# Two transformer layers on one core: the output projection of the two-layer steps, dimension-major against token-major in units of 32 tokens

## The chip, the cores and the metric

The kernel runs on one core of a Trainium2 chip. A core has a matrix engine (PE, with its weight loads PEld listed apart), a vector engine (DVE), a scalar engine (ACT), a general engine (POOL) and a queue engine that issues transfers (SP). PE reads from the large on-chip memory and writes its results into accumulation banks (PSUM), of which the kernel uses eight, each of 512 fp32 columns over 128 partitions. DVE and ACT read the banks and write back to the large memory. The metric is the device time of one execution in microseconds; less is better.

## The reference, cut to what matters

Two layers, each of an attention over segments with a recurrent memory and of a gated feed-forward part. There are 2048 tokens of 448 dimensions, 16 heads of width 256, 64 segments of 32 tokens, and 8 memory tokens. A segment's memory is the projected output of the segment before it at the memory's places:

```python
for s in range(n_seg):
    h = jnp.concatenate([mem, xs], axis=1)          # 8 + 32 tokens
    q, k, v = h @ Wq, h @ Wk, h @ Wv                # per head
    p = softmax(mask(q k^T * scale))
    o = einsum('bhte,hed->btd', p v, Wo)
    mem = o[:, :M, :]                               # goes into the next segment
    outs.append(o[:, M:, :])
...
x = x + A(layernorm(x)); x = x + B(layernorm(x))    # B: relu(x Wg) * (x Wu) then Wd
x = x + A(layernorm(x)); x = x + B(layernorm(x))
```

The same weights serve both layers. The 64 steps of the memory are a chain: no segment can begin its memory part before the one ahead of it has projected its output.

## The kernel before

**Weights.** Once, at the start, the kernel multiplies Wq with Wk and Wv with Wo per head (`A_sb`, `A3`, `A3z` for the scores, `B_sb` for the output). After that, each head's attention works on the hidden vectors themselves. `B_sb[:, hf, t, :]` holds, for half `hf` of the heads (0 or 1) and tile `t` of 28, a 128 x 448 block of the fused output weight.

**Steps.** `step(g, ff)` (L751) handles segment `g` of layer 1 ("chain 0") and segment `g - 4` of layer 2 ("chain 1") together; there are 68 steps, and those with g from 4 to 63 have both chains. Every odd step also carries a `Feed` (L466): residual, layer norm and feed-forward of one block of 64 tokens of each layer, and loading and storing of those blocks. A step's order on PE is written out by hand, since every matmul is chained to the one before (`in_order`, L74). On the other engines the planner orders instructions by when their inputs are ready, except where `keep_in_program_order` pins an instruction behind the one traced before it on its engine.

**Inside a two-chain step.** Twelve banks of projections (`prj`), whose results ACT and DVE copy to `TQ` and `TZ`; scores of the memory tokens (`Sm`) and of the segment (`Sx`), softmax on DVE and ACT; weighing of the hidden vectors by the probabilities (`weigh_m`, `weigh_m_rows`, `weigh_x`: tiles `ya`, `yb`, `ym`, `y`), whose results are copied into `Y` or `Z`; and the output projection. `YY[hf]` is a pair of buffers, Y for even steps and Z for odd ones, each of 28 tiles by 80 columns: 32 of chain 0, 16 of memory tokens (from `M0` = 32), 32 of chain 1. The segment's columns are written at the end of a step for the next step (`kept`, L844), the memory's in the step itself.

**The output projection before.** `project_out` (L877) has the weight as the stationary operand and 80 columns of `Y` as the moving one: 28 tiles x 2 halves x 3 blocks of 128 output dimensions, 168 matmuls into one bank `ox`. `project_tail` (L929) does the last 64 dimensions in 56 matmuls on two column halves of the array, into the bank `o3`, with copies by ACT and additions by DVE to bring the halves together. The output comes out dimension-major, so the memory tokens can be copied straight into the next step's input `hT` (`finish`, L950; `set_mem`, L228; `project_tail` for the last dimensions). The segment's output goes to `OT`, and at the next odd step `flip_out` (L479) transposes it back on PE, so that `residual` (L482) adds it to the tokens. `weigh_x(1, ...)` is the last thing that a step puts on PE, behind the projection.

**What lies beside.** In an odd step the projection is dealt out between the pieces of the feed-forward part: 10 tiles ahead of `gate_up`, the tail ahead of `down`, the rest behind `down`, with `flipped(PX[1])`, `norm2` and `feed_on` in between (L1113 to L1141). In an even step it stands in four pieces (L1162 to L1179). Banks come from a pool of seven (`ps`) and one more with the tag `ox`, which the projection's bank shares with the bank `c0` of projections and with one of the two banks that `flip_banks` (L176) takes.

**Token-major code that is there already.** The last step does its output in units of 32 tokens on four column tiles, with 32 tokens of `Y` or `Z` stationary and 224 columns of `B_sb` moving (`project_tokens` L962, `add_tokens` L972). Each of its two units has a bank of its own. Steps 1 to 3, which have one chain, project 40 tokens at a time on two column tiles (`project_rows` L891) and transpose the result back on PE (`finish_rows` L918).

Of the kernel before, what the change touches and what calls it, by code (L numbers as in the profile page):

```python
# [54 lines left out]
def build_kernel(ctx, tc, A_x, A_mem0, A_Wq, A_Wk, A_Wv, A_Wo, B_W_gate, B_W_up, B_W_down, out,  # L55
# [29 lines left out]
    def tr(*a):  # L85
        in_order(nc.tensor.transpose(*a))  # L86
# [89 lines left out]
    def flip_banks():  # L176

        return [psum.tile([P, 8, 64], BF, name=f"flip{r}", **where)
                for r, where in enumerate((dict(tag="ox", bufs=1), dict(tag="ps")))]

    def flipped_dims(two, at, src):

# [35 lines left out]
    def rows_in(eng, b, c, src):  # L218

        x = slice(HX[c], HX[c] + SEG)  # L220
        evac(eng, chunks(b)[:, :, 0:4, x].transpose([0, 2, 1, 3]), src.rearrange("p k (s t) -> p k s t", t=SEG))

    def mem_cols(g, cs):
        b, j = divmod(g, BLK)
# [1 line left out]
        return h[:, :, cs[0]:cs[-1] + 1, 0:MEM]  # L226

    def set_mem(g, src, cs, n=4):  # L228
        nc.vector.tensor_copy(mem_cols(g, cs)[:, 0:n], src)


    def idle(n):
# [217 lines left out]
    YY = [[main.tile([P, NT, W], BF, name=f"{name}{hf}") for name in "YZ"] for hf in range(2)]  # L450
    for hf in range(2):
        nc.gpsimd.memset(YY[hf][0][:, :, 0:SEG], 0.0)
    xT = main.tile([P, NPASS, 128], BF, name="xT")
# [8 lines left out]

    part = main.tile([P, 2, DM], F32, name="part")


    class Feed:  # L466

# [21 lines left out]
        def norm(self, eng=None):  # L489
            self.xn = normed(self.st, eng)  # L490

        def xposed(self, other=None):
            tps = transpose_tokens(self.xn)
            r = nc.vector.tensor_copy(xT[:, 0:4, self.n], tps[:, :, self.n])
            if other is not None:
                behind(r, other)
            return tps

        def xposed_rest(self, tps, pin=False, rs=(0, 1)):
            for r in rs:  # L500
                i = nc.scalar.copy(xT[ROWS[r], 4:NPASS, self.n], tps[ROWS[1 - r], 0:3, self.n])
                if pin:
                    tc.keep_in_program_order(i)

        def gate_up(self, u):
            n = self.n
            gps = psum.tile([P, 2, 128], F32, tag="ps", name="gps")
            ups = psum.tile([P, 2, 128], F32, tag="ps", name="ups")
            for i in range(NPASS):
                for e in range(2):  # L510
                    f = 2 * u + e
                    for r, ps in enumerate((ups, gps)):
                        mm(ps[:, e, n], Wgu_sb[ROWS[r], i, f * 128:(f + 1) * 128], xT[ROWS[r], i, n],
                           start=(i == 0 and e == 0), stop=(i == NPASS - 1), skip_group_check=True)
# [236 lines left out]
    def step(g, ff):  # L751
# [5 lines left out]
        cols = [(0, 32) if c == 0 else (48, 80) for c in xs] + [(32, 40) if c == 0 else (40, 48) for c in ms]  # L757
        lo, hi = min(a for a, _ in cols), max(b for _, b in cols)
        if g == 0:
            lo = 0  # L760
# [8 lines left out]
            return YY[hf][(g + later) % 2]  # L769

        def flips_of_rows():
            two = flip_banks()
# [40 lines left out]
        def weigh_m(hf, hk, PT):  # L813
            if not ms:
                return
            ya = psum.tile([P, 256], F32, tag="ps", name="ya")
            for kd in range(2):
                mm(ya[:, kd * 128:kd * 128 + 128], hk[:, kd, :], PT[:], start=True, stop=True)
            nc.scalar.copy(ys(hf)[:, 0:16, M0:M0 + 16], ya[:].rearrange("p (t q) -> p t q", q=16))  # L819
# [4 lines left out]
            nc.vector.tensor_copy(ys(hf)[:, 16:28, M0:M0 + 16], yb[:].rearrange("p (t q) -> p t q", q=16))  # L824

        def weigh_m_rows(hf, hk, PT):
            pt = PT[:, 0:128].rearrange("p (t c m) -> p t c m", c=2, m=MEM)
            y = {c: psum.tile([P, NT * MEM], F32, tag="ps", name=f"ym{c}") for c in ms}
            for kd in range(3):
                for c in ms:  # L830
                    rows = slice(64 * c, 64 * c + L)
                    mm(y[c][:, kd * 64:kd * 64 + 64], hk[rows, kd, :], pt[rows, :, c, :], start=True, stop=True)
            for eo in range(2):
                for c in ms:
                    rows = slice(64 * c, 64 * c + L)
                    mm(y[c][:, 192:224], hk[rows, 4 + eo, :], pt[rows, 4 * eo:4 * eo + 4, c, :], start=(eo == 0),
                       stop=(eo == 1))
            for c in ms:
                evac(nc.scalar if c == 0 else nc.vector, ys(hf)[:, :, M0 + MEM * c:M0 + MEM * c + MEM],
                     y[c][:].rearrange("p (t m) -> p t m", m=MEM))  # L840

        def weigh_x(hf, hk, PT):

            kept = ys(hf, 0 if last else 1)  # L844
            xo = (None, XO[1] - SEG) if g == nseg + LAG - 2 else XO

            def keep(eng, c, t0, src):
                n = src.shape[-1] // SEG
                dst = kept[:, t0:t0 + n, xo[c]:xo[c] + SEG]
                k = max(1, n // 8)  # L850
                r = evac(eng, dst.rearrange("p (k i) (e q) -> p k e i q", k=k, q=16),
                         src.rearrange("p (k e i q) -> p k e i q", k=k, e=2, q=16))
                if eng is nc.vector and hf == 1 and t0 == 0:
                    tc.keep_in_program_order(r)
# [13 lines left out]
            for c in chains:  # L868
                keep(nc.scalar if c == 0 else nc.vector, c, 16, y2[c][:, 0:256])
                tail = y2[c][:, 256:512].rearrange("p (o e i q) -> p e i o q", o=2, e=2, i=4)  # L870
                for e in range(2):
                    rows = slice(64 * e, 64 * e + 64)
                    evac(nc.vector if c == 0 else nc.scalar,
                         kept[rows, 24:28, xo[c]:xo[c] + SEG].rearrange("p i (o q) -> p i o q", q=16),
                         tail[rows, e])

        def project_out(hf, t0, t1):  # L877

# [39 lines left out]
        def finish_rows(mt):  # L918
# [2 lines left out]
            for kd in range(4):  # L921
                tr(tps[:, kd, 0:L], mt[0:L, kd * 128:kd * 128 + 128], ident[0:L, 0:L])
            if ms:
                m = M0 + MEM * ms[0] - lo
                set_mem(g + 1, tps[:, :, m:m + MEM].unsqueeze(2), ms)
            for x, ot in outs():
                nc.vector.tensor_copy(ot, tps[:, :, x.start - lo:x.stop - lo])

        def project_tail():  # L929

# [6 lines left out]
            nc.scalar.copy(swap[0:64, lo:hi], o3[64:128, lo:hi])  # L937
            nc.scalar.copy(swap[64:128, lo:hi], o3[0:64, lo:hi])
            if ms:
                both = slice(M0 + MEM * ms[0], M0 + MEM * (ms[-1] + 1))  # L940
# [8 lines left out]

        def finish():  # L950
            if ms:
                src = ox[:, :, M0:M0 + 16].rearrange("p k (c m) -> p k c m", m=MEM)
# [114 lines left out]
            ff.xposed_rest(tps, True, (0,))  # L1067
        if len(chains) == 2:
            Sx0 = scores_x(0)
            weigh_m(0, hk, pm)  # L1070
            if ff is not None:
                ff.xposed_rest(ff.xposed())
            scores_m(1)
            Sx1 = scores_x(1)
# [1 line left out]
        else:  # L1076
# [7 lines left out]
            Sx1 = scores_x(1)  # L1084
            weights_end(*half0)
        load_piece()
        if ff is not None and rows:
            project_rows(0, 0, 8)
            half1 = begin_x(1, Sx1)
# [160 lines left out]
```

## Time and profile before

| what | value |
|---|---|
| device time, median of 3 runs (lowest to highest) | 1527.6 us (1526.77 to 1528.19) |
| the profiled execution: its own time, its span | 1527.14 us, 1525.4 us |
| PE busy | 1513.0 us, 99% of the span |
| PE weight loads busy | 1393.9 us, 91% |
| DVE, ACT, POOL busy | 1047.4 us, 806.0 us, 164.5 us |
| one even step with two chains (699.54 to 717.18 us) | 17.64 us |
| one odd step with two chains (717.18 to 743.51 us) | 26.33 us |
| granted clock of PE over the span | 0.999 |

A step is taken here from the first projection of a step (`prj<-hT,A`, 12 matmuls) to that of the next. In the window of these two steps PE is busy 43.97 of 43.97 us, DVE 30.42, ACT 23.12, POOL 4.59. Matmuls overlap and their ends are modelled, so a group's cost on PE is read from its start to the start of what follows it, not from its duration.

### The profile page before, as it was taken

How to read it: one execution, taken by the hardware profiler on the slowest of the kernel's cores; microseconds unless marked ns; L12 is line 12 of the kernel's file. 1: busy time of each engine (PE TensorE's matmuls, PEld its weight loads, DVE VectorE, ACT ScalarE, POOL GpSimd, SP SyncE). 2: the span in 40 equal slices, each digit the busy share in tenths (PEclk: the TensorE clock that was granted, in tenths of full speed). 3: DMA queues.
4: the chain of work that ended last, by engine and by line, in shares of the span. 5: the costliest groups of instructions: out<-in, count | busy, mean ns of one | idle time of the engine just before them, and what ended most of it. 6: DMA issues, size and time to landing. Idle time of an engine off the chain costs nothing.

```text
span 1525.4 us, 96313 instructions
## 1 busy us (share of the span) xinstructions
PE 1513.0 (99%) x44178; PEld 1393.9 (91%) x44178; DVE 1047.4 (69%) x3787; ACT 806.0 (53%) x2358; POOL 164.5 (11%) x310
## 2 busy tenths in 40 slices
PE   9999999999999999999999999999999999999998
PEld 7678999999999999999999999999999999999987
DVE  6856676677666666766676776666766766666765
ACT  6645555555545555554455455545555655455444
POOL 4000111101101111011011101100111011011100
PEclk9999999999999999999999999999999999999999
DMA  8810000000000000000000000000000000000002
GB/s 259 239 34 9 9 10 10 10 4 10 10 10 10 10 11 9 6 10 10 10 10 10 10 4 10 10 10 10 10 10 8 6 9 10 10 9 7 7 7 79
DMA packets 30406, 35.76 MB, mean 23 GB/s; under 512 B 3560, under 2 KB 28336, under 8 KB 30000
## 3 DMA queue, kind: packets, MB, share of 16 engines
q1 hardware_dynamic: 29936, 29.60, 7.0%
q8 instruction: 345, 5.65, 1.6%
q14 instruction: 61, 0.50, 0.1%
q0 software_dynamic: 64, 0.01, 0.0%
HBM read 25.93 MB, written 1.84 MB: 18 GB/s over the span
## 4 chain that ended last, share of the span: by engine, by line
PE 98%; DVE 1%; ACT 1%; DMA 0%; issue 0%; POOL 0%; ACTq 0%; DVEq 0%; POOLq 0%; SPq 0%
PE prj L83 31%; PE ox L83 25%; PE ups L83 11%; PE dps L83 6%; PE o L83 5%; PE y L83 4%; PE Sx L83 3%; PE bps L83 1%; PE Sm L83 1%; PE aps L83 1%; PE pps L86 1%; PE or L83 1%; PE gps L83 1%; PE tps L86 1%; PE flip L86 1%; PE ym L83 1%
## 5 line engine op out<-in xcount | busy, mean ns | idle before, releaser
L83 PEld LDWEIGHTS <-B_sb 128*128 128x128 bf16 (+1 forms) x14336 | 465.7, 103 | 22.1 <-issue 14.6
L83 PE MATMUL prj<-hT,A_sb 128*128 128x80 bf16 (+1 forms) x11256 | 429.3, 200 | 1.1 <-issue 1.1
L83 PEld LDWEIGHTS <-A_sb 128*128 128x128 bf16 x11424 | 413.0, 100 | 9.0 <-issue 1.4
L83 PE MATMUL ox<-Y,B_sb 128*128 128x80 bf16 (+2 forms) x5544 | 213.5, 200 | 0.6 <-ACT Y L819 0.5
L83 PE MATMUL ox<-Z,B_sb 128*128 128x80 bf16 (+1 forms) x5208 | 203.9, 201 | 0.2 <-ACT Z L819 0.2
L107 ACT CAST TQ<-prj 128x480 bf16<-128x480 f32 (+3 forms) x414 | 175.8, 469 | 14.6 <-PE prj L83 3.2
L83 PE MATMUL ups<-xT,Wgu_sb 64*128 64x128 bf16 (+1 forms) x3136 | 182.8, 214 | 0.2 <-issue 0.2
L83 PE MATMUL gps<-xT,Wgu_sb 64*128 64x128 bf16 (+1 forms) x3136 | 182.9, 214 | 0.0
L108 DVE CAST TQ<-prj 128x480 bf16<-128x480 f32 (+3 forms) x353 | 137.9, 425 | 65.0 <-PE prj L83 64.9
L83 PEld LDWEIGHTS <-Wgu_sb 64*128 64x128 bf16 x6328 | 176.7, 94 | 3.0 <-issue 0.9
L107 ACT CAST Z<-y 64x128 bf16<-64x128 f32 (+2 forms) x263 | 91.4, 374 | 137.7 <-PE y L83 85.8
L107 ACT CAST TZ<-prj 64x320 bf16<-64x320 f32 (+2 forms) x292 | 111.0, 388 | 77.9 <-PE prj L83 73.2
L516 ACT CAST ut<-ups 128x256 bf16<-128x256 f32 (+1 forms) x224 | 81.7, 366 | 78.9 <-PE gps L83 62.4
L517 DVE SCALAR_TENSOR_TENSOR hh<-gps,ut 128x256 bf16<-128x256 f32 (+1 forms) x224 | 90.2, 414 | 45.2 <-ACT ut L516 32.9
L107 ACT CAST Y<-y 128x512 bf16<-128x512 f32 (+1 forms) x252 | 87.6, 375 | 59.8 <-DVE Y L108 58.8
L107 ACT COPY hT<-tps 128x256 bf16<-128x256 bf16 (+1 forms) x32 | 11.8, 369 | 187.2 <-DVE hT L108 180.8
L108 DVE CAST Y<-y 128x512 bf16<-128x512 f32 (+1 forms) x252 | 102.5, 417 | 8.4 <-ACT Y L107 2.9
L108 DVE CAST Z<-y 64x128 bf16<-64x128 f32 (+2 forms) x257 | 101.8, 417 | 8.8 <-ACT Z L107 3.5
L710 ACT ACTIVATE se<-se 128x80 f32<-128x80 f32 (+2 forms) x270 | 69.7, 292 | 43.4 <-DVE se L709 41.0
L718 DVE TENSOR_REDUCE ssum<-se 128x2 f32<-128x80 f32 (+2 forms) x270 | 68.3, 268 | 34.7 <-ACT se L710 33.5
L83 PE MATMUL dps<-Wd_sb,hh 128*128 128x448 bf16 (+2 forms) x490 | 90.7, 348 | 0.0
L195 POOL TENSOR_SCALAR rstd<-mv 128x1 f32<-128x1 f32 x67 | 15.3, 228 | 689.5 <-DVE mv L193 689.4
(159 smaller groups left out, 2253.2 us busy)
## 6 DMA issues: line engine op xcount, KB each, us to landing
wo<-in_A_Wo_dram SPq DMA_DIRECT2D x8, 448.0 KB, 6.1
Wgu_sb<-in_A_Wq_dram SPq DMA_DIRECT2D x8, 384.0 KB, 5.0
Wgu_sb<-in_A_Wk_dram SPq DMA_DIRECT2D x8, 384.0 KB, 4.7
Wgu_sb<-in_A_Wv_dram SPq DMA_DIRECT2D x6, 384.0 KB, 6.4
xa<-in_A_x_dram SPq DMA_DIRECT2D x32, 56.0 KB, 2.2
xa<-xp SPq DMA_DIRECT2D x32, 56.0 KB, 1.9
out_dram<-xa SPq DMA_DIRECT2D x31, 56.0 KB, 3.0
xp<-in_A_x_dram SPq DMA_DIRECT2D x30, 56.0 KB, 2.1
```

Source lines behind the costliest of these rows:

```text
L83: in_order(nc.tensor.matmul(*a, **k))
L86: in_order(nc.tensor.transpose(*a))
L107: return nc.scalar.copy(dst, src)
L108: return eng.tensor_copy(dst, src)
L195: nc.gpsimd.tensor_scalar(out=rstd[:], in0=mv[:, 1:2], scalar1=EPS, scalar2=None, op0=ALU.add)
L516: nc.scalar.copy(ut[:, :, n], ups[:, :, n])
L517: nc.vector.scalar_tensor_tensor(out=hh[:, 2 * u:2 * u + 2, n], in0=gps[:, :, n], scalar=0.0, in1=ut[:, :, n], op0=ALU.max, op1=ALU.mult)
L710: nc.scalar.activation(se, se, AF.Exp, scale=SCALE)
L718: nc.vector.tensor_reduce(ssum, se, axis=AX.X, op=ALU.add)
```

## The change

Steps 5 to 62 (`split(g)`) get another output projection.

- **Units.** The stationary operand is now 32 tokens of `Y` or `Z`, the moving one half of the output dimensions (224 columns of `B_sb`). A unit of 32 tokens takes 112 matmuls, of which four at a time go to the four column tiles of the array (partitions 0, 32, 64 and 96). All units of a step accumulate in one bank `ox`, in its columns 0 to 223 or 224 to 447.
- **Half a segment held over.** Per pair of steps there are 160 tokens, which is five units: three in the even step, two in the odd one. An even step's `weigh_x` puts the first 16 tokens of chain 1 into its own buffer (columns 32 to 47), where the next even step finds them, and the other 16 into the next step's buffer (48 to 63). The memory tokens stand at 48 to 63 in even steps and at 32 to 47 in odd ones (`mem_at`), so that columns 32 to 63 are a full unit, memory included. Other tokens of chain 1 stand at 64 to 95 of the even buffer, which grows to 96 columns.
- **Gathering.** Each of a unit's output halves lies on two column tiles (even and odd tiles `t`). `gather_unit` copies one pair of strips with ACT and adds with two or three DVE instructions. The two further units of an even step sum over all tiles on one column tile each and are copied out by `leave_two`, two pieces with ACT and two with DVE.
- **Memory back.** `memory_on` transposes the unit that holds the memory on PE (four transposes) and `set_mem` copies it into `hT`.
- **Residual.** The rows lie in `AT` token-major, so from step 7 on `residual` is one addition, and `flip_out` is left out; in the even step both flip banks come from `ps`.
- **Order.** Odd: `begin_x(1)`, `gate_up` 0 to 2 with no projection ahead of them, end of the softmax, `gate_up` 3, one transposition of five blocks, and so on; the whole projection stands behind `down`. `ff.xposed` stands ahead of `weigh_m(0)`, and `xT` is split into `xT` and `xR`. Even: the unit with the memory for half 0, then the other two units up to tile 16; five blocks of probabilities are transposed into one bank and copied out by DVE, ACT and DVE in turn; tiles 17 to 21 of the two units; `weigh_m_rows(1)`, `weigh_x(0)`; the memory's unit for half 1 and its `gather_unit`; the rest of the two units; `leave_two`, `memory_on`, `weigh_x(1)`. Some instructions are pinned.

The diff, cut to its core:

```diff
+    AT = main.tile([P, 512], BF, name="AT")
+    MT = main.tile([2 * SEG, 512], BF, name="MT")
...
         def residual(self):
+            if not later_flips(2 * self.i + 3):
+                nc.vector.tensor_tensor(self.x[:], AT[:, 0:DM], self.x[:], op=ALU.add)
+                self.st = row_stats(self.x)
+                return
...
         def feed_on(self):
             if self.first:
                 tps = transpose_tokens(self.xn)
-                rows_in(nc.vector, self.i + 2, 1, tps[:, :, TB:P])
+                tc.keep_in_program_order(rows_in(nc.vector, self.i + 2, 1, tps[:, :, TB:P]))
                 if self.i < nblk - 1:
-                    rows_in(nc.scalar, self.i + 2, 0, tps[:, :, 0:TB])
+                    tc.keep_in_program_order(rows_in(nc.scalar, self.i + 2, 0, tps[:, :, 0:TB]))
...
+            def places(c):
+                if c == 1 and split(g + 1):
+                    if g % 2 == 0:
+                        return [(ys(hf), 32, slice(0, 1)), (kept, 48, slice(1, 2))]
+                    return [(kept, 64, slice(0, 2))]
+                return [(kept, xo[c], slice(0, 2))]
...
+        def open_units():
+            nonlocal ox
+            ox = psum.tile([P, 512], F32, tag="ox", bufs=1, name="ox")
+
+        def unit(q, hf, t, a, at, d, first):
+            mm(ox[q:q + 32, at:at + HALF], ys(hf)[:, t, a:a + 32], B_sb[:, hf, t, HALF * d:HALF * d + HALF],
+               start=first, stop=(hf == 1 and t >= NT - 2), tile_position=(0, q), skip_group_check=True)
+
+        def unit_in_pairs(a, q0, at, hf, first=False):
+            for t in range(0, NT, 2):
+                for e in range(2):
+                    for d in range(2):
+                        unit((q0 + 64 * e + 32 * d) % P, hf, t + e, a, at, d, first and hf == 0 and t == 0)
+
+        def two_units(hf, t0, t1):
+            for t in range(t0, t1):
+                for a, q in ((64, 32), (0, 96)):
+                    for d in range(2):
+                        unit(q - 32 * d, hf, t, a, HALF, d, False)
+
+        def gather_unit(q0, at, dst, dup):
+            other = main.tile([P, 3, HALF], F32, tag="sums0", name="sums")[:, 0, :]
+            q1 = 64 - q0
+            yield nc.scalar.copy(other[q0:q0 + 64, :], ox[q1:q1 + 64, at:at + HALF])
+            yield nc.vector.tensor_tensor(dst[:, 0:HALF], ox[q0:q0 + 32, at:at + HALF], other[q0:q0 + 32, :], op=ALU.add)
+            hi2 = slice(q0 + 32, q0 + 64)
+            n = 384 - HALF if dup else HALF
+            yield nc.vector.tensor_tensor(dst[:, HALF:HALF + n], ox[hi2, at:at + n], other[hi2, 0:n], op=ALU.add)
+            if dup:
+                yield nc.vector.tensor_tensor(
+                    dst[:, 384:512].rearrange("p (k d) -> p k d", d=64),
+                    ox[hi2, at + n:at + HALF].unsqueeze(1).to_broadcast([32, 2, 64]),
+                    other[hi2, n:HALF].unsqueeze(1).to_broadcast([32, 2, 64]), op=ALU.add)
+
+        def leave_two(d):
+            for eng, q in ((nc.vector if d == 0 else nc.scalar, 32), (nc.vector if d == 0 else nc.scalar, 96)):
+                yield evac(eng, AT[q:q + 32, HALF * d:HALF * d + HALF], ox[q - 32 * d:q - 32 * d + 32, HALF:2 * HALF])
+
+        def memory_on(mt):
+            tps = psum.tile([P, 4, 64], BF, tag="ps", name="tpr")
+            for kd in range(4):
+                tr(tps[:, kd, :], mt[0:64, kd * 128:kd * 128 + 128], ident[0:64, 0:64])
+            m = 0 if g % 2 else 16
+            return set_mem(g + 1, tps[:, :, m:m + 16].rearrange("p k (c m) -> p k c m", m=MEM), ms)
...
             Sx0 = scores_x(0)
+            if ff is not None and split(g):
+                ff.xposed_rest(ff.xposed(None, True), True)
             weigh_m(0, hk, pm)
-            if ff is not None:
+            if ff is not None and not split(g):
                 ff.xposed_rest(ff.xposed())
...
+        if split(g) and ff is not None:
+            half1 = begin_x(1, Sx1)
+            feed(0, 1, 2)
+            weights_end(*half1)
+            feed(3)
+            pt = flipped_rows([(PM[1], 1), (PX[0], 2), (PX[1], 2)])
+            feed(4)
+            weigh_m_rows(1, hk, pt)
+            feed(5, 6)
+            weigh_x(0, hk, pt[:, 128:384])
+            ff.down()
+            open_units()
+            for hf in range(2):
+                unit_in_pairs(32, 0, 0, hf, True)
+            pinned(gather_unit(0, 0, AT[0:32], True))
+            ff.norm2()
+            for hf in range(2):
+                unit_in_pairs(0, 64, HALF, hf)
+            ff.feed_on()
+            pinned([memory_on(AT)])
+            pinned(gather_unit(64, HALF, AT[64:96], False))
+            ff.leave()
+            weigh_x(1, hk, pt[:, 384:640])
+            return
+        if split(g):
+            half1 = begin_x(1, Sx1)
+            open_units()
+            unit_in_pairs(32, 0, 0, 0, True)
+            two_units(0, 0, 17)
+            weights_end(*half1)
...
+            two_units(0, 17, 22)
+            weigh_m_rows(1, hk, pt[:, 0:128])
+            weigh_x(0, hk, pt[:, 128:384])
+            load_piece()
+            unit_in_pairs(32, 0, 0, 1)
+            pinned(gather_unit(0, 0, MT[0:32], True))
+            nc.gpsimd.tensor_copy(AT[0:16, 0:DM], MT[0:16, 0:DM])
+            two_units(0, 22, NT)
+            two_units(1, 0, NT)
+            pinned(leave_two(1))
+            a = leave_two(0)
+            pinned([next(a)])
+            pinned([memory_on(MT)])
+            pinned([next(a)])
+            weigh_x(1, hk, pt[:, 384:640])
+            return
```

More of the change, by code (lines that the diff above doesn't have):

```diff
@@ L449, in build_kernel @@
     swap = main.tile([P, W], F32, name="swap")
-    YY = [[main.tile([P, NT, W], BF, name=f"{name}{hf}") for name in "YZ"] for hf in range(2)]
+    YY = [[main.tile([P, NT, W + 16 * (i == 0)], BF, name=f"{name}{hf}") for i, name in enumerate("YZ")]
+          for hf in range(2)]
     for hf in range(2):
-        nc.gpsimd.memset(YY[hf][0][:, :, 0:SEG], 0.0)
-    xT = main.tile([P, NPASS, 128], BF, name="xT")
+        nc.gpsimd.memset(YY[hf][0][:, :, 0:2 * SEG], 0.0)
+    AT = main.tile([P, 512], BF, name="AT")
+    MT = main.tile([2 * SEG, 512], BF, name="MT")
+    for t in (AT, MT):
+        nc.gpsimd.memset(t[:], 0.0)
+    xT = main.tile([P, 4, 128], BF, name="xT")
+    xR = main.tile([P, 3, 128], BF, name="xR")
     hh = main.tile([P, FT, 128], BF, name="hh")
@@ L463, in build_kernel, with split, later_flips, mem_at @@
     part = main.tile([P, 2, DM], F32, name="part")
+    def split(g):
+        return LAG < g <= nseg - 2
+    def later_flips(g):
+        return not (split(g - 1) and split(g - 2))
+    def mem_at(g):
+        return 48 if g % 2 == 0 and LAG <= g <= nseg - 2 else M0
     class Feed:
@@ L490, in norm, with xposed @@
             self.xn = normed(self.st, eng)
-        def xposed(self, other=None):
+        def xposed(self, other=None, pin=False):
             tps = transpose_tokens(self.xn)
-            r = nc.vector.tensor_copy(xT[:, 0:4, self.n], tps[:, :, self.n])
+            r = nc.vector.tensor_copy(xT[:, :, self.n], tps[:, :, self.n])
+            if pin:
+                tc.keep_in_program_order(r)
             if other is not None:
@@ L500, in xposed_rest @@
             for r in rs:
-                i = nc.scalar.copy(xT[ROWS[r], 4:NPASS, self.n], tps[ROWS[1 - r], 0:3, self.n])
+                i = nc.scalar.copy(xR[ROWS[r], :, self.n], tps[ROWS[1 - r], 0:3, self.n])
                 if pin:
@@ L771, in flips_of_rows @@
         def flips_of_rows():
-            two = flip_banks()
+            two = flip_banks(g % 2 == 0 and split(g - 1))
             kps = flipped_dims(two, 0, lambda r, kd: hb[ROWS[r], j, kd * HI:kd * HI + HI])
-            if ff is not None:
+            if ff is not None and later_flips(g):
                 ff.flip_out(two)
@@ L872, in weigh_x @@
                     rows = slice(64 * e, 64 * e + 64)
-                    evac(nc.vector if c == 0 else nc.scalar,
-                         kept[rows, 24:28, xo[c]:xo[c] + SEG].rearrange("p i (o q) -> p i o q", q=16),
-                         tail[rows, e])
+                    for to, at, h in places(c):
+                        evac(nc.vector if c == 0 else nc.scalar,
+                             to[rows, 24:28, at:at + 16 * (h.stop - h.start)].rearrange("p i (o q) -> p i o q", q=16),
+                             tail[rows, e, :, h])
         def project_out(hf, t0, t1):
@@ new lines, in leave_two, with pinned @@
+        def leave_two(d):
+            for eng, q in ((nc.vector if d == 0 else nc.scalar, 32), (nc.vector if d == 0 else nc.scalar, 96)):
+                yield evac(eng, AT[q:q + 32, HALF * d:HALF * d + HALF], ox[q - 32 * d:q - 32 * d + 32, HALF:2 * HALF])
+        def pinned(its):
+            for i in its:
+                tc.keep_in_program_order(i)
+        def memory_on(mt):
[4 more added lines that the diff above has]
+            return set_mem(g + 1, tps[:, :, m:m + 16].rearrange("p k (c m) -> p k c m", m=MEM), ms)
@@ L1086, in step @@
         load_piece()
+        if split(g) and ff is not None:
[28 more added lines that the diff above has]
+            weights_end(*half1)
+            pps = psum.tile([P, 5, 128], BF, tag="ps", name="pps")
+            for b, (src, k) in enumerate(((PM[1], 0), (PX[0], 0), (PX[0], 1), (PX[1], 0), (PX[1], 1))):
+                tr(pps[:, b, :], src[:, 2 * k:2 * k + 2, :], ident[:])
+            pt = main.tile([P, 640], BF, tag="PTr5", name="PT")
+            for b0, b1, eng in ((0, 1, nc.vector), (1, 3, nc.scalar), (3, 5, nc.vector)):
+                tc.keep_in_program_order(evac(eng, pt[:, 128 * b0:128 * b1], pps[:, b0:b1, :].rearrange("p b q -> p (b q)")))
+            two_units(0, 17, 22)
[13 more added lines that the diff above has]
+            weigh_x(1, hk, pt[:, 384:640])
+            return
         if ff is not None and rows:
```

34 lines of the change are left out of this document (20 added, 14 removed).

## The prediction

> **What bounds the kernel now.** I read the page's busy times first, then its chain that ended last:
>
> ```profile
> PE 1513.0 (99%) x44178; PEld 1393.9 (91%) x44178; DVE 1047.4 (69%) x3787; ACT 806.0 (53%) x2358; POOL 164.5 (11%) x310
> ...
> PE 98%; DVE 1%; ACT 1%; DMA 0%; issue 0%; POOL 0%; ACTq 0%; DVEq 0%; POOLq 0%; SPq 0%
> ```
>
> PE never waits to speak of. The time is the sum of what stands on PE, and it changes in two ways only: PE's work gets shorter, or PE begins to wait. So I read PE's timeline over an even step, the end of an odd one, and the last step, which has units of 32 tokens already (columns: start, length, engine, line, operation, shapes, count):
>
> ```profile
> 708.43 2.63 PE L83 MATMUL ox<-Y,B_sb 128*128 128x80 bf16 x69
> ...
> 711.06 0.70 PE L83 MATMUL ox<-Y,B_sb 128*128 128x80 bf16 x15
> 711.70 0.30 PE L83 MATMUL ym<-PT,hk 40*128 40x64 bf16 x10
> 711.85 0.60 PE L83 MATMUL y<-PT,hk 40*128 40x256 bf16 x8
> 712.38 1.19 PE L83 MATMUL o<-Y,B_sb 128*64 128x80 bf16 x56
> 713.50 1.90 PE L83 MATMUL ox<-Y,B_sb 128*128 128x80 bf16 x48
> ```
> ```profile
> 742.23 0.44 PE L86 MATMUL tps<-ident,xn 128*128 128x128 bf16 x4
> 742.51 0.59 PE L83 MATMUL ox<-Z,B_sb 128*128 128x80 bf16 x12
> 743.03 0.61 PE L83 MATMUL y<-PT,hk 40*128 40x256 bf16 x8
> 743.51 0.39 PE L83 MATMUL prj<-hT,A 64*128 64x80 bf16 x12
> ```
> ```profile
> 1505.86 0.85 PE L83 MATMUL ot<-B_sb,Z 128*32 128x224 bf16 x28
> 1506.65 0.61 PE L83 MATMUL y<-PT,hk 40*128 40x256 bf16 x4
> 1507.19 2.20 PE L83 MATMUL ot<-B_sb,Z 128*32 128x224 bf16 x84
> 1509.32 0.40 PE L86 MATMUL tps<-ident,xn 128*128 128x128 bf16 x4
> ```
>
> A run costs the distance from its start to the next one's. For waits I asked for the tile `tps`, whose bank DVE and ACT both read in disjoint columns, and for the end of the odd step:
>
> ```profile
> L501 ACT COPY xT<-tps x64: 311/472/477, 118.3 to 1469.7; 64x384 bf16<-64x384 bf16 x60, 64x192 bf16<-64x192 bf16 x4
> ...
> its engine sat idle before it (us, times) until:
>   DVE hT L108: 180.8, 31
> ...
>   DVE xT L494: 11.8, 30
> ```
> ```profile
> 742.71 0.29 DVE L108 COPY hT<-tps 128x256 bf16<-128x256 bf16 x1 [0.32 <-PE tps L86]
> ...
> 743.09 0.37 ACT L107 COPY hT<-tps 128x256 bf16<-128x256 bf16 x1 [6.18 <-DVE hT L108]
> ```
>
> Nothing in the arithmetic ties ACT's copy to DVE's, yet ACT waited for it every time: engines that use one bank take turns, whichever columns they use. This row decides my forecast.
>
> **The change, per pair of steps.** Steps 5 to 62 make 29 pairs.
>
> *A, the projection itself.* Before, the five runs of `ox` and `o` in the even step cost 2.46 + 0.64 + 1.12 + 1.73 + 1.38 = 7.33 us by starts; those in the odd step 7.34. Units: 28 matmuls cost 0.79 us (1505.86 to 1506.65), 84 cost 2.13, so the 56 between cost 1.34 and a group of four 0.096; the first run's rest of 0.12 is the price of entering the form. A unit of 28 groups is 2.68 us; five are 13.42, and four entries add 0.48. 14.67 becomes 13.90: -0.77.
>
> *B, transposes.* The odd step's flips shrink from 16 (0.34 us) to 8 (0.22): -0.12. Its later `pps` pair goes, 0.11, and four more blocks in `ppr` cost 0.06 (six took 0.09). `memory_on` adds four transposes to each step: 0.15 to 0.3 us with the entry, 0.2 taken, 0.4 for both. Sum +0.2, between 0 and 0.4.
>
> *C, the odd step's first gather.* PE writes unit 32, ACT and DVE read its strips out of bank `ox`, and PE's next unit goes into the same bank, other columns, all four strips. By the turns above PE waits until the last addition has read. The last step prices the reads: PE left unit `ot` at 1510.43, ACT's copy ran from 1510.50 (0.342 us), DVE's addition (64x224, 0.383) from 1510.90 to 1511.28. Two more additions, of 160 and 128 columns, step like the 128x160 fp32 ones (0.32 long, 0.23 apart): 0.5. With 0.05 to PE, 1511.83 - 1510.43 = 1.4. DVE and ACT are free by then: residual sums and statistics end about 2 us after `down`, and the unit takes 2.68. No row shows a matmul entering a bank that others are reading; from below the cost is 0 (first rival), from above 1.6. I take 1.4, since the nearest rows, readers of one bank, never overlap. Behind the waiting matmul stands everything on PE.
>
> *D, the even step's gather.* The same 1.4, and the gather's copy is pinned behind ACT's last copy of `weigh_x(0)`. Before, `y` began at 711.85 and these copies ended at 713.95, 2.1 later; chain 1's are now cut in two, four pieces more at 0.2 or less on each engine's share, so some 2.6. PE needs 0.53 (`y`) + 1.34 (half a unit) + 0.12 = 2.0, so ACT is late by 0.5 to 0.6. Taken 1.9, between 0 and 2.3.
>
> *E, the odd step's end.* From `tps` to the next projection the chain is PE, DVE copy, ACT copy: 742.23 to 743.51, 1.28 us, covered exactly by `tps` 0.28, 12 `ox` 0.52 and `y` 0.48. The 12 `ox` go and four transposes (0.15) come: 0.37 uncovered; between 0 and 0.6.
>
> *F, the odd step's middle.* Thirty `ox` (1.16 us from 726.40) go from between the scores and `gate_up`. They covered DVE's softmax, which ran until 729.51, and ACT's `xT` copies, until 727.52. `xposed`, moved ahead of `weigh_m(0)`, is four transposes (0.22), one DVE and two ACT copies and no transfer; `ya` and `yb` get behind them, without harm, as their columns are read only after `down`. With `xR` apart only the DVE copy (0.41) must be in for the first 16 matmuls. But `gate_up` also needs two of seven banks, and the score bank leaves with the subtraction at 726.89: about 0.3 late. `flipped_rows` now needs `PX[1]` too; with two `hh` (0.34 apart) squeezed ahead it is ready near 729.9, about when PE gets there. Taken 0.4, between 0 and 0.8.
>
> *G, the even step's end.* Memory went from `ox` by one DVE copy, 0.2, under `y`, 0.45. Now one leaving copy on DVE (0.33) stands ahead of `set_mem`: late by 0.1. If DVE's copies take turns with ACT's two (0.34 each), it is 0.85. Taken 0.3.
>
> At nothing: the other additions, `AT`, the single residual (0.55 on DVE for 0.37; `xn` has 0.9 us of room before `tps`, from 724.52 to 725.40), POOL's row copy (0.27), and the wider memsets at the start, which end before the first memory copy into `Y`; uncovered, some 0.3 a pair and 2 us once. SP's queue keeps its order: the four transfers of a block are issued behind the same sums.
>
> Sum: -0.77 + 0.2 + 1.4 + 1.9 + 0.37 + 0.4 + 0.3 = +3.8; times 29 = +110 us. The profiled execution took 1527.14 us (span 1525.4 and 1.7 around it), within 0.5 of the median of 1527.6. Forecast **1637 us**. With C from 1.2 to 1.6, D from 1.4 to 2.3 and the others partly at their ends, +1.9 to +5.3 a pair: 1582 to 1682.
>
> [...]
>
> **The rivals.**
> - *Gathers run beside the units.* If a matmul may write a bank that others read, C and D vanish: +0.5 a pair, 1542. For it: the tails of PE's work behind each gather (2.68 and 3.3 us) would cover the reads. Against it: the `tps` rows. 0.09.
> - *Faster.* The same, and E, F and G are hidden as well: -0.57 a pair, 1511. One mechanism decides, whether PE must wait for a reader of bank `ox`; without it the other waits have to stay under 0.57 a pair together. For it: before, such waits were all covered to the tenth. 0.10.
> - *One gather waits, or a part of each* (the additions' strips are free earlier, or the planner gets the copies out sooner): about +2.1 a pair, 1588. 0.09.
> - *The units lose their rate in the middle of the kernel*, and the projection costs what it did: with covered waits no change. The 21 groups in a row at 1507 kept 0.096 us. 0.03.
>
> **How the numbers follow.** The forecast has 0.69. Its own range, 1582 to 1682, holds nine tenths of that. Down to 1540 comes the third rival and over half of the first, above I go to 1685: about 8 in 10. Faster by over 0.2% (which is about what a measurement of this kernel tells from no change): 0.10. Within 0.2%: 0.03. Slower: the rest, 0.87.
>
> **What would show it.** In the changed profile: units at 0.096 us a group (A); PE idle ahead of `ox` twice a pair, released by the DVE additions of `gather_unit`, 1.4 us in odd and 1.9 in even steps (C, D); idle ahead of the first `prj` of even steps, released by ACT `hT` (E), and of `ups` by DVE `se` (F). PE's busy time should go down, its share of the span to about 91%. The prediction is wrong if matmuls of the next unit start while the gather still reads, or if E to G outweigh C and D.

## The result, and the profile after

The changed kernel takes **1740.1 us** (median of 4 runs, 1739.56 to 1742.54) against 1527.9 beside it (4 runs, 1526.77 to 1528.96): a ratio of 1.139, 95% interval 1.137 to 1.141. It is 13.9% slower, where the forecast was 7% and the range ended at 1685.

The page's busy times and its chain that ended last, of the changed kernel:

```profile
PE 1568.7 (90%) x47484; PEld 1380.5 (79%) x47484; DVE 1100.6 (63%) x3816; ACT 856.5 (49%) x2532; POOL 183.8 (11%) x341
...
PE 75%; ACT 11%; DVE 11%; issue 3%; DMA 0%; SPq 0%; ACTq 0%; POOL 0%; DVEq 0%
```

PE, which held 98% of that chain before, now stands on three quarters of it; ACT and DVE have 11% each. The span grew by 212.4 us, to 1737.8, and PE is idle for 169 us of it (12 before). PE's busy time grew too, from 1513.0 to 1568.7 us. PE's waits by releaser (columns: who waited, for whom, us in total, times, longest):

```profile
PE ox L83 <- DVE MT L1002: 64.4, 29, 2.3
PE ox L83 <- DVE AT L1002: 40.3, 29, 1.4
PE prj L83 <- DVE hT L229: 23.1, 31, 0.8
PE prj L83 <- ACT hT L107: 5.6, 29, 0.5
PE gps L83 <- ACT xR L523: 5.5, 28, 0.2
PE ym L83 <- DVE PT L108: 5.5, 28, 0.2
```

L1002 is the last addition of `gather_unit`, into `MT` in even steps and into `AT` in odd ones. Each stops PE 29 times, once a pair. The two runs of units, on PE's timeline, even step first:

```profile
803.31 0.61 PE L83 MATMUL y<-PT,hk 40*128 40x256 bf16 x8
804.03 1.52 PE L83 MATMUL ox<-B_sb,Y 128*32 128x224 bf16 x56
807.80 3.44 PE L83 MATMUL ox<-B_sb,Y 128*32 128x224 bf16 x136 [2.25 <-DVE MT L1002]
811.18 0.23 PE L86 MATMUL tpr<-ident,MT 64*128 64x64 bf16 x2
...
811.30 0.60 PE L83 MATMUL y<-PT,hk 40*128 40x256 bf16 x7
812.70 0.39 PE L83 MATMUL prj<-hT,A 64*128 64x80 bf16 x12 [0.79 <-DVE hT L229]
...
832.25 2.87 PE L83 MATMUL ox<-B_sb,Z 128*32 128x224 bf16 x112
836.51 2.87 PE L83 MATMUL ox<-B_sb,Z 128*32 128x224 bf16 x112 [1.39 <-DVE AT L1002]
839.31 0.40 PE L86 MATMUL tps<-ident,xn 128*128 128x128 bf16 x4
```

The second run of each step, though it goes into other columns of `ox`, begins only after the gather's last addition. On DVE and ACT the even step's gather reads so:

```profile
805.80 0.20 ACT L107 CAST Y<-y 64x64 bf16<-64x64 f32 x1 [1.22 <-DVE Z L108]
...
806.23 0.21 ACT L107 CAST Z<-y 64x64 bf16<-64x64 f32 x1
806.47 0.34 ACT L996 COPY sums<-ox 64x224 f32<-64x224 f32 x1
811.32 0.68 ACT L107 CAST AT<-ox 32x224 bf16<-32x224 f32 x2 [4.51 <-PE ox L83]
```
```profile
805.43 0.28 DVE L108 CAST Z<-y 128x128 bf16<-128x128 f32 x1
806.84 0.38 DVE L997 TENSOR_TENSOR MT<-ox,sums 32x224 bf16<-32x224 f32 x1 [1.13 <-ACT sums L996]
807.23 0.32 DVE L1000 TENSOR_TENSOR MT<-ox,sums 32x160 bf16<-32x160 f32 x1
807.48 0.27 DVE L1002 TENSOR_TENSOR MT<-ox,sums 32x128 bf16<-32x128 f32 x1
812.04 0.38 DVE L108 CAST AT<-ox 32x224 bf16<-32x224 f32 x1 [4.29 <-ACT AT L107]
812.45 0.19 DVE L229 COPY hT<-tpr 128x64 bf16<-128x64 bf16 x1
```

ACT's copy for the gather, at 806.47, stands behind four small copies of `y`, and these had waited 1.22 us for DVE to leave the same bank. At the end of the step DVE's first leaving copy (812.04) waits for ACT's two (811.32 to 812.00), and the memory's copy to `hT` (812.45) stands behind that.

One loss has another form. In nine even steps the units behind the wait run at half speed. The next lines show such a step and then an ordinary one, each in two stretches: the run of units ahead of the wait together with the wait, and the run behind it (columns: start and end, us, then busy us and instructions of PE, PEld, DVE, ACT, POOL, then the granted clock, the transfers' share and GB/s):

```profile
905.30:909.10 3.80, 1.54 (x60) 1.30 (x61) 2.49 (x9) 1.54 (x7) 0.00 (x0) 1.00 0.02 4
909.10:912.60 3.50, 3.50 (x80) 3.13 (x84) 0.00 (x0) 0.00 (x0) 0.55 (x1) 0.52 0.02 5
...
804.00:807.90 3.90, 1.62 (x60) 1.40 (x64) 2.50 (x9) 1.56 (x7) 0.02 (x1) 1.00 0.00 0
807.90:811.20 3.30, 3.30 (x137) 3.12 (x135) 0.00 (x0) 0.00 (x0) 0.53 (x1) 1.00 0.02 5
```

In 909.10 to 912.60 the granted clock is 0.52, and 80 matmuls pass in 3.50 us where 137 pass in 3.30 us otherwise.

The account of an undisturbed pair, from the starts of PE's matmuls in both traces. A wait is longer here than in the list above (1.55 against 40.3/29 = 1.39, 2.41 against 64.4/29 = 2.22), since the profile counts a matmul as busy to its modelled end, also when nothing follows it:

| part | before | after | difference |
|---|---|---|---|
| projection without its waits (`ox`, `o`) | 14.67 | 13.93 | -0.74 |
| runs that stand beside units, whole (all four `Sx`, `dps`, both `tps`) | 4.74 | 5.10 | +0.36 |
| transposes `tpr`, `ppr`, odd `pps`, odd flips, without waits | 0.60 | 0.64 | +0.04 |
| wait behind the odd gather | | 1.55 | +1.55 |
| wait behind the even gather | | 2.41 | +2.41 |
| odd step's end (`y`, even flips) | | | +0.52 |
| around `gate_up` (0.74 in it, 0.29 at `ppr`) | | | +1.03 |
| even step's end (`y`, `prj`) | | | +1.24 |
| even step's middle (`pps`, `ym`, `y`) | | | +0.33 |
| pair | 43.91 | 50.64 | +6.73 |

Over 29 pairs 6.73 us make 195; the nine stretches at half clock add 1.66 each, 15 us; the steps ahead of step 5 and behind step 62 add about 3. Together some 213, for 212.4 measured. Without any of the waits (the -0.74, +0.36 and +0.04 alone) a pair would be 0.34 us shorter than before.

### The profile page after: what moved, and what is told of

It reads as the page before. It is cut to its first block, busy times and chain, and to the rows that moved or that the text cites. A ratio compares the mean times of both kernels' runs of the same rounds, so it can differ in the third digit from the quotient of the medians.

```text
span 1737.8 us, 103419 instructions
## 1 busy us (share of the span) xinstructions
PE 1568.7 (90%) x47484; PEld 1380.5 (79%) x47484; DVE 1100.6 (63%) x3816; ACT 856.5 (49%) x2532; POOL 183.8 (11%) x341
## 4 chain that ended last, share of the span: by engine, by line
PE 75%; ACT 11%; DVE 11%; issue 3%; DMA 0%; SPq 0%; ACTq 0%; POOL 0%; DVEq 0%
PE prj L83 28%; PE ox L83 24%; PE dps L83 5%; PE ups L83 3%; PE Sx L83 2%; DVE hh L540 2%; ACT Z L107 2%; ACT xR L523 2%; DVE Z L108 1%; PE y L83 1%; PE bps L83 1%; ACT Y L107 1%; PE aps L83 1%; ACT sums L996 1%; ACT AT L107 1%
## 5 line engine op out<-in xcount | busy, mean ns | idle before, releaser
L83 PE MATMUL ox<-B_sb,Y 128*32 128x224 bf16 x9744 | 269.7, 268 | 67.4 <-DVE MT L1002 64.4
L83 PEld LDWEIGHTS <-Y 128*32 128x32 bf16 (+1 forms) x9856 | 241.0, 100 | 91.9 <-DVE MT L1002 71.8
L83 PEld LDWEIGHTS <-Z 128*32 128x32 bf16 (+1 forms) x6944 | 163.8, 97 | 63.3 <-DVE AT L1002 47.7
L83 PE MATMUL ox<-B_sb,Z 128*32 128x224 bf16 x6496 | 166.3, 259 | 40.3 <-DVE AT L1002 40.3
L108 DVE CAST Y<-y 64x128 bf16<-64x128 f32 (+1 forms) x368 | 144.0, 399 | 10.8 <-ACT Y L107 2.7
L83 PE MATMUL ups<-xT,Wgu_sb 64*128 64x128 bf16 (+1 forms) x1792 | 133.3, 214 | 2.9 <-DVE hh L540 0.3
L83 PE MATMUL ups<-xR,Wgu_sb 64*128 64x128 bf16 (+1 forms) x1344 | 113.8, 215 | 0.2 <-issue 0.2
L83 PE MATMUL gps<-xR,Wgu_sb 64*128 64x128 bf16 (+1 forms) x1344 | 108.8, 214 | 5.6 <-ACT xR L523 5.5
L83 PE MATMUL prj<-hT,A 64*128 64x80 bf16 (+1 forms) x3216 | 80.0, 196 | 28.8 <-DVE hT L229 23.1
L83 PEld LDWEIGHTS <-A 64*128 64x128 bf16 x3216 | 69.9, 96 | 41.1 <-issue 36.2
```

The costliest lines, as they stand in the source:

```text
L83: in_order(nc.tensor.matmul(*a, **k))
L108: return eng.tensor_copy(dst, src)
```

## The experiments

The theory at this point: PE waits wherever it enters a bank whose readers have not finished (1.55 and 2.41 us a pair), readers of one bank take turns (ACT's copies of `y` waited 1.22 us for DVE's), and the half clock (nine times, 3.41 us each) follows the longest of these waits. The rivals: the waits have some other cause (data, a late buffer); the half clock belongs to the new form of matmul; DVE and ACT simply have too much to do. Each time below is that of one execution; the kernel before took 1529.2 us beside the first four kernels and 1527.8 beside the other three. The four runs of the changed kernel lie within 3 us, so a difference of a few us is read from the lengths of steps in the traces rather than from the time. In this section a step runs from its first flip (`flip<-ident,hT`) to the next step's: so taken, the changed kernel's odd step is 27.54 us and its undisturbed even step 23.10.

**A bank of its own for the memory unit.** The edit:

```diff
             ox = psum.tile([P, 512], F32, tag="ox", bufs=1, name="ox")
+            ou = psum.tile([P, 512], F32, tag="ps", name="ou")
...
-            mm(ox[q:q + 32, at:at + HALF], ys(hf)[:, t, a:a + 32], B_sb[:, hf, t, HALF * d:HALF * d + HALF],
+            mm((ox if at else ou)[q:q + 32, at:at + HALF], ys(hf)[:, t, a:a + 32], B_sb[:, hf, t, HALF * d:HALF * d + HALF],
...
+            o = ox if at else ou
-            yield nc.scalar.copy(other[q0:q0 + 64, :], ox[q1:q1 + 64, at:at + HALF])
+            yield nc.scalar.copy(other[q0:q0 + 64, :], o[q1:q1 + 64, at:at + HALF])
```

The additions read `o` likewise, and the units in `ox` now start their own sums.

> The changed kernel, but a step's memory unit gets a bank of its own, so that no matmul goes into a bank that a gather reads. If PE waits for the readers of its bank, both waits ahead of `ox` (1.55 us in odd and 2.41 us in even steps over 29 pairs: 115 us) go, and with them the nine stretches of half clock (15 us): 1740 falls to about 1610. If the matmuls behind the gather wait for something else (data, a late buffer of Y or Z), they go on waiting and the time stays near 1740. One bank less in the pool may cost some 5 to 10 us elsewhere.

It took 1618.4 us, 121.7 less. Nothing changed in the data, the order or the amount of copying, and PE has one bank less in the pool. Both waits are gone from the list. The first line below is now its longest, and the last is new:

```profile
PE prj L83 <- DVE hT L229: 23.4, 31, 0.8
...
PE ox L83 <- issue: 5.4, 14, 0.8
```

The odd step falls from 27.54 to 25.97 us, the even one from 23.10 to 20.6 (its commonest length); between step 5 and step 62 no half clock is left. So the bank makes the two waits, not the data. (A tile of the units fills a whole bank, so the runs don't tell a wait by bank from a wait by tile.) The run fell 8 us short of what was expected; the last line shows why in part: PE now pauses inside some runs of units with nothing to wait for that the profile shows. The cause of these pauses stays open.

**Eight idle transposes in the even step's wait.** The edit:

```diff
+            idle(8)
             two_units(0, 22, NT)
```

> The changed kernel with 8 idle transposes (about 0.45 us) in the even step's wait, into a bank of their own. They lie inside the wait, so they cost nothing by themselves. If half clock is granted after a window of 3.41 us in which PE idled for more than about 2 us, the largest idle share falls from 2.25 to 1.8 us, no stretch of half clock is left and the time falls by 15 us to about 1725. If the drops have another cause (the units' form, the time since the last drop), nine of them stay and the time is 1740.

`idle(8)` transposes the identity eight times into a bank that nobody reads. The run took 1722.7 us, 17.4 less, for 8 matmuls *more* per even step. The granted clock of the whole run rose from 0.990 to 0.999, and no stretch of half clock is left from the first step to the last. The list shows the wait shorter by 0.55 us a step (64.4 to 48.4 us in 29 steps), where the transposes had been put at 0.45:

```profile
PE ox L83 <- DVE MT L1002: 48.4, 29, 1.7
PE ox L83 <- DVE AT L1002: 40.3, 29, 1.4
```

The units ran in the same form as before, so the half clock follows from the idling and not from the form.

**Memory ahead of the leaving copies.** The edit:

```diff
-            pinned(leave_two(1))
-            a = leave_two(0)
-            pinned([next(a)])
             pinned([memory_on(MT)])
-            pinned([next(a)])
+            pinned(leave_two(1))
+            pinned(leave_two(0))
```

> The changed kernel, but in even steps the memory is transposed and copied ahead of the four copies of leave_two. If set_mem was late because DVE's first leaving copy took its turn behind ACT's two, the wait at the even step's end (1.25 us a pair) goes: about 1740 - 36 = 1704, less or more by up to 15 us as the steps' length shifts against the clock's windows. If only DVE's own copy (0.38 us) was in the way, 1740 - 11 = 1729.

It took 1747.3 us, 7.2 *more*. The memory came in time: `y` at the even step's end fell from 1.39 to 0.44 us and the wait for `hT` L229 left the list. But another took its place at once:

```profile
PE ox L83 <- DVE MT L1002: 64.3, 29, 2.3
PE ox L83 <- DVE AT L1002: 40.3, 29, 1.4
PE flip L86 <- ACT Z L107: 23.7, 29, 0.8
```

The next step's flips want a bank, and ACT's copy that frees one stands behind the leaving copies. An undisturbed even step became shorter by 0.26 us only (22.84), and with that length the waits fell more often into the clock's windows (3.41 us each, as the last section reads them): 17 stretches of half clock in the whole trace instead of 10, a mean clock of 0.983. Both expectations missed: the leaving copies were in the way of two things, and taking one out of their way was worth 0.26, not 1.25.

**Half the memory unit ahead of `gate_up`.** The edit:

```diff
             half1 = begin_x(1, Sx1)
+            open_units()
+            unit_in_pairs(32, 0, 0, 0, True)
             feed(0, 1, 2)
...
-            open_units()
-            for hf in range(2):
-                unit_in_pairs(32, 0, 0, hf, True)
+            unit_in_pairs(32, 0, 0, 1)
```

> The changed kernel, but in odd steps half of the memory unit (56 matmuls, 1.34 us) stands ahead of gate_up 0 instead of behind down. If the waits around gate_up and flipped_rows (1.05 us a pair) come from the projection's cover having gone, they fall to 0.1 or 0.2: about -26 us, with one more entry of 0.12 (+3.5 us): 1717. If DVE's amount of work is what limits that stretch, the waits move on behind the unit and the time stays within 5 us of 1740.

It took 1743.8 us, 3.7 more, though the odd step fell from 27.54 to 27.07: `gate_up` went from 6.22 to 5.87 us and `ppr` from 0.44 to 0.15, and the projection had one more entry (7.06 to 7.24). The 0.47 us a pair are worth 14 us, somewhat over half of the 23 that were expected, and were eaten by the clock: 17 even steps at half clock instead of 9, and two more stretches outside them. By the time alone this would have looked like the rival; the steps' lengths say that the cover was part of the cause. What is left in `gate_up`, 0.39 us, is one wait, `weigh_m_rows` for the copy of `PT`.

**Two banks and another end of the even step.** The edit, beside two banks (in odd steps the second unit takes the bank from the pool):

```diff
-            two_units(0, 17, 22)
+            two_units(0, 17, NT)
...
-            two_units(0, 22, NT)
-            two_units(1, 0, NT)
...
-            weigh_x(1, hk, pt[:, 384:640])
+            two_units(1, 0, 22)
+            pinned([memory_on(MT)])
+            two_units(1, 22, NT)
+            weigh_x(1, hk, pt[:, 384:640], lambda: (pinned(leave_two(1)), pinned(leave_two(0))))
```

The last argument is called between the copies of `y1` and the matmuls of `y2`; the odd step's flips take both banks from the pool.

> Two banks as in the run with two banks (1618 us), and another end of the even step: the memory is transposed and copied with six tiles of the two units still to come, the four copies of leave_two come behind the first copies of weigh_x(1), both flip banks of the odd step come from the pool, and weigh_m_rows stands behind 11 tiles of units. If the 1.25 us at the even step's end were the memory's place behind copies that take turns, they go, with 0.2 us at weigh_m_rows: 1618 - 29 x 1.4 = 1577. If the engines' copies are simply too many there, the wait moves to the next bank that PE needs, and the time stays above 1600.

It took 1613.1 us, 5.3 less than with two banks alone, where 41 had been expected. The even step fell, from 20.6 to 19.75 us, but the odd step rose from 25.97 to 26.84: its flips took 0.61 instead of 0.22 us and its projections 7.73 instead of 7.24. The pause in the projections ends with ACT's last copy out of a bank of `y`. The second case on record holds: the wait moved to the next banks, and the time stayed above 1600. In this kernel the late copies cost about as much at the one place as at the other.

**Two banks and an earlier `feed_on`.** The edit:

```diff
-            for hf in range(2):
-                unit_in_pairs(0, 64, HALF, hf, True)
+            unit_in_pairs(0, 64, HALF, 0, True)
+            unit_in_pairs(0, 64, HALF, 1, True, 0, 18)
             ff.feed_on()
+            unit_in_pairs(0, 64, HALF, 1, True, 18, NT)
```

> Two banks as in the run with two banks (1618 us), and feed_on with ten tiles of units still to come. If the wait ahead of the odd step's end (0.33 us in `y` and `prj`, 0.19 at the flips) is the chain from `tps` over DVE's copy to ACT's copy, it goes, and one more entry of the units (0.12) comes: 29 x 0.4 less, 1607. If it is the memory's own way (gather, transposes, set_mem), nothing changes: 1618.

It took 1608.9 us, 9.5 less than with two banks, 11 expected. The odd step's two runs of `y` fell together from 1.34 to 1.00 us and the wait for ACT's copy to `hT` left the list, so that chain was the cause of that part. But the flips that follow grew from 0.41 to 0.70 us, waiting for another bank:

```profile
PE prj L83 <- DVE hT L229: 23.5, 31, 0.8
PE flip L86 <- ACT Y L107: 8.9, 29, 0.6
```

With 0.12 for the new entry the earlier `feed_on` gained nothing: -0.34 + 0.12 + 0.28 is +0.06 us a pair. An undisturbed pair is shorter by 0.13 us (46.55 to 46.42) for another reason. This run takes its banks as the run before it does, with both flip banks of odd steps from the pool, and not as the first run with two banks, so the odd step's flips begin 0.22 us behind the step's first projection instead of 0.43. The remaining 6 us of the 9.5 lie in pauses inside the units and in the first steps. That the time came near the expected 1607 is chance.

**All of it.** The other end of the even step and the earlier `feed_on` together, with two banks, half the memory unit ahead of `gate_up`, and `weigh_m_rows` behind `gate_up` 5.

> Both of these, and half of the memory unit ahead of gate_up, with weigh_m_rows behind gate_up 5. If the waits are as the traces put them, a pair loses 1.4 at the even end, 0.4 at the odd end and 0.8 to 1.0 around gate_up against the 46.84 us with two banks: 44.1 us and about 1540 us. The units' saving of 0.76 us a pair shows as a time under 1527.6 only if fewer than 0.5 us of waits and changes of form are left. If DVE and ACT have too much to do, the time stays above 1565.

It took 1590.4 us, where 1540 had been expected. `gate_up` is back at 5.48 us, its length before the change, and a pair takes 45.73 us instead of the expected 44.1. Against the 43.91 of before, the projection is 0.44 us shorter (its gain of 0.74 less three more entries), the runs beside the units are 0.36 longer, the memory's transposes cost 0.45, the other transposes save 0.18, and some 1.67 us of waits are left: 0.85 at the flips of both steps, 0.49 in the odd step's projections, 0.33 in the even step's middle. By their releasers most of them are for banks:

```profile
PE flip L86 <- ACT Y L107: 8.9, 29, 0.6
PE flip L86 <- ACT Z L107: 6.1, 29, 0.2
PE ou L83 <- DVE Y L108: 4.7, 29, 0.2
PE ov L83 <- issue: 2.5, 6, 0.6
```

Even without those waits the pair would take some 44.1 us, not less than before. The time also lies above the 1565 us that the record names for the rival, that DVE and ACT have too much to do. Over the whole span neither is full (DVE 70%, ACT 54%), but no run took copies away, so it stays open whether the order of the copies or their number makes the waits that are left. No version that was run beats the kernel before the change.

## Why the prediction was wrong, point by point

The direction, the mechanism and both places of the two long waits were right; the sum was too small, 110 us where 212 came. By its own steps:

- **A, -0.77 a pair: held.** -0.74, and a group of four kept 0.096 us outside the half clock. What it left out is the price on the other side of the form: the run ahead of a unit or behind it also grows, 0.36 a pair in all.
- **B, +0.2: held** within its bounds (+0.04).
- **C, 1.4: held** (1.55). The bank was the cause, as the run with two banks shows. (The last step's row was read 0.05 us early: ACT's copy began at 1510.55, which makes the sum 1.43.)
- **D, 1.9: right in kind, mis-sized,** 2.41 and just above its upper bound of 2.3. The backlog on ACT was counted as more and smaller copies, 2.6 us behind the start of `y`; it ended 3.1 behind it (806.44), since ACT's four last copies also waited 1.22 us for DVE in one bank. The turns that the forecast stood on were not counted at the copies ahead of the gather.
- **E, 0.37: 0.52.** The chain through DVE's and ACT's copies was right (the earlier `feed_on` took its 0.34 out of `y`); a wait for a bank at the flips, 0.19, came on top, and grew when the chain was shortened.
- **F, 0.4: 1.03.** Above its bound of 0.8. Three things came late in turn. In the first `gate_up` the matmuls behind the first 16 wait for ACT's copies to `xR` (0.37 by the starts); the prediction had looked at the first 16 alone. The one behind `ppr` waits for DVE's `hh` (0.29). `weigh_m_rows` waits for the copy of `PT` (0.37). None of them is the forecast wait of `ups` for DVE's `se`. Moving 1.34 us of units ahead took away the first two, for 0.18 of a new entry, and `weigh_m_rows` one `gate_up` later the third.
- **G, 0.3: 1.24.** The working had a price close by, 0.85 if DVE's copies take turns with ACT's, and chose the low one. The turns made the memory late by some 0.95; the other 0.3 is the next step's flips, which wait for DVE's second leaving copy. The trace shows the turns although the four copies read different 32-partition strips (ACT ended at 812.00, DVE began at 812.04). So this program's waits went by the whole bank, or by the tile that fills it, here as at C and D (40.3 and 64.4 us in PE's list).
- **At nothing:** the runs beside the units, under A, and the even step's middle had no term (0.36 and 0.33). The middle has five blocks in one bank, copied by DVE, ACT and DVE in turn.
- **The clock had no term.** 15 us of the 212 come from half clock behind the longest wait, and nothing in the trace of before, with its 0.999, would have shown it.
- **A sign that failed:** PE's busy time was to go down and went up by 55.7 us. About 15 of these are half clock. The rest, some 1.4 us a pair by this difference, fits the way in which the profile counts: each stop of PE adds the modelled end of the matmul ahead of it to the busy time.

The step that failed is the reading of the other waits as things that could be covered: E, F, G and the middle were given 1.07 a pair together and took 3.12, which is 59 us of the 102 that the forecast lacked. Engines that take turns at banks and copies that stand behind others made them longer, and in three of the four runs that took one away the next one grew (memory first, the other end of the even step, the earlier `feed_on`). The rest of the 102 is D with 15 us, the clock with 15, the runs beside the units with 10, and small differences. The rivals' times were wrong in the same way: without C and D the kernel takes 1618 us, not 1542.

## What to carry to other kernels

In a program whose waits go by the bank, as here, count the reading of a part of a bank as a wait of the engine that fills another part: the units behind the gathers went into other columns and still waited 1.55 and 2.41 us a pair. Two readers took turns here as well, in other partitions too (DVE from 812.04 us, behind ACT's copies until 812.00): add these turns, and the copies queued ahead of them. Before work is moved out from behind a wait, list what else it covered, and expect a removed wait to come back at the next bank. And a form of matmul with a 5% better rate (13.93 us a pair for 14.67) has to be set against every change into it and out of it: here the 0.74 us a pair stood against 0.36 at the borders and 0.2 to 0.45 for the memory's transposes.

## What the runs showed of the hardware that was not expected

In the changed kernel each stretch of half clock between the first step and the last lasts 3.41 us, and all of them begin on a fixed grid of 3.41 us: the starts of the nine stand 153.60 us apart, 45 times 3.4133. Laid over PE's idle time of the changed kernel, the nine windows of that grid with 2.10 us of idling or more are exactly those that a stretch of half clock follows, and the three with the next most, 1.88 to 1.89 us, are followed by none. With half the unit ahead of `gate_up`, all windows from 1.96 us up are followed by one, and that with 1.94 is not; with the memory first, those from 2.15, while one with 1.99 is not. With eight transposes the largest has 1.70, and none is. So a wait of 2.25 us, far shorter than the window but lying wholly in it, was enough. Between step 5 and step 62 of these four runs the least idling that a stretch followed was 1.96 us of 3.41, and the most that none followed 1.99.

Some stretches this count does not explain: with two banks, with the memory first and with all of it there is one near step 4, behind windows with 1.42, 1.72 and 1.77 us of idling, and in the last of these one more among the last steps, behind 1.59 us. Among the last steps there is also one with half the unit ahead, behind 1.41 us, and one of two windows' length with the memory first, behind 0.90 us. What the clock goes by at these places stays open.

A window with work in 38% of it (2.10 of 3.41 us idle, the least of the nine) was enough for the drop. The grid also explains the regular pattern: in the changed kernel three pairs, one of them 1.66 us longer, take 153.6 us, just 45 windows, so that the same phase comes back every third pair.
